# A decode step on one core: TensorE's program made shorter with register-addressed loops, q and h computed with the weights as stationary operand, one V buffer

## The chip, the cores and the metric

The kernel runs on one core of a Trainium2 chip. The metric is the device time of one execution in microseconds (us), lower is better. The kernel before takes 112.35 us (median of three runs, 112.1 to 112.72). In the later sections it was run again beside every experiment on the same chip, and its medians there are 111.36 to 112.28. Because of this spread, I give for every experiment its excess: its median less the median of the kernel before in the same call.

TensorE is the matrix engine. The profile shows its work as loads of a stationary operand ("load") and matmuls that stream a moving operand through it ("matmul"), 558 of each in the kernel before; one load and one matmul are called a pair here, and one run through a loop's body a pass. The granted clock is the share of TensorE's full clock that the profile shows it to have had. VectorE does the elementwise work, the transposes and the copies out of the accumulators in these kernels. A transfer queue (SP in the profile) issues the loads from memory.

## The reference, cut to what matters

```python
def reference(A_x, A_k_cache, A_v_cache, A_wq, A_wo, B_x, B_w1, B_w2):
    # B=2, Sq=1, D=448, 16 query heads, 8 K/V heads, Dh=256; the last W=2048 keys of 8192
    xn = _layernorm(A_x)
    q = (xn @ wq)                       # 448 x 4096
    scores = einsum(q, k[-2048:]) / 16
    o = softmax(scores) @ v[-2048:]
    s = o.reshape(B, 1, 4096) @ wo      # 4096 x 448
    g = silu(relu(xn @ w1) @ w2)        # the FFN: 448 x 1792, 1792 x 448
    return A_x + s * g
```

Nearly all of the work is reading 44 MB: 16.8 MB of K, 16.8 MB of V, and 10.6 MB of wq, w1, w2 and wo.

## The kernel before

The keys and values are treated in four units u = 0 to 3 of 4.2 MB of K and 4.2 MB of V each (one batch element, four K/V heads). For each unit VectorE transposes K (T), TensorE makes the scores (S), softmax follows, TensorE spreads P over the partitions (the P products), and P times V (PV) is summed. TensorE's part of a unit is one body of a loop over "turns", in which PV lags by one turn and the small products after PV (turn, spread) by two. A token is a semaphore that is counted down when it is taken, so that the same wait can stand in every turn.

The products of q, of h (x times w1) and of F (h times w2) have x or h as the small stationary operand and the weights as the moving one, 448 or 512 columns at a time:

```python
        def load_v(u, cuts=(0, NT)):          # units 0 to 2 in vbuf[0], unit 3 in vbuf[1], where wq was
            deps = [None if u == 0 else st["q_mm"] if u == NU - 1 else st["PV", u - 1]]
            ...
        d_wq = [pr.dma(SP, wq_sb[:, 0:FIRST * HC], wq_src[:, 0:FIRST * HC])]       # 2/7 of wq
        load_k(0)
        d_wq.append(pr.dma(SP, wq_sb[:, FIRST * HC:SLOTS * HC], wq_src[:, FIRST * HC:SLOTS * HC]))
        load_k(1)
        load_v(0)
        st["w1"] = pr.dma(...)                # right behind V0
        st["w2"] = pr.dma(...)
        ...
            for x in range(4):                # softmax(u): the P products, 16 pairs, written out
                for g in range(4):
                    lo = 128 * (4 * x + g)
                    o = pr.op(PE, mm(view(pbk, 2 * x, [[8, 16], [1, 2]]), spread[:, lo:lo + 128], ...
        ...
        def do_q():                           # 28 pairs, written out
            for s in range(SLOTS):
                for i in range(4):
                    lo = s * HC + i * 512
                    o = pr.op(PE, mm(obk[32 * i:32 * i + 4, :], xr[:, 4 * s:4 * s + 4], wq_sb[:, lo:lo + 512], ...
        ...
            if u == 1:                        # the FFN stands at the end of turn 1
                pr.group = "ffn"
                do_H()                        # 28 pairs
                do_F()                        # 14 pairs
        ...
        turn(3)
        v_f = pr.op(DVE, ...)
        idle_loop(5, 2)                       # ten matmuls whose result nobody reads
        do_PV(3, (0, 1))
        attend_turn(2)
        do_PV(3, (2,))
        attend_spread(2)
        do_PV(3, (3,))
        ...
        idle_work(1)
        ...
        idle_work(3)
```

Of the kernel before, what the change touches and what calls it, by code (L numbers as in the profile page):

```python
# [14 lines left out]
class _Op:  # L15
    __slots__ = ("eng", "fn", "deps", "dma", "needed", "value", "sem", "turn", "group", "token", "gives")

    def __init__(self, eng, fn, deps, dma):
        self.eng, self.fn, self.deps, self.dma = eng, fn, deps, dma
        self.needed, self.value, self.sem = dma, 0, None  # L20
        self.turn, self.group, self.token, self.gives = None, None, None, False


class _Prog:
# [4 lines left out]
    def __init__(self, nc, es):  # L29
        self.nc, self.es = nc, es  # L30
        self.lists = {PE: [], DVE: [], ACTE: [], SP: [], POOL: []}
        self.turn, self.group, self.runs = None, None, {}

    def op(self, eng, fn, deps=(), token=None):
        o = _Op(eng, fn, [d for d in deps if d is not None], False)
        if eng == PE:
            o.turn, o.group, o.token = self.turn, self.group, token
        self.lists[eng].append(o)
        return o
# [6 lines left out]
    def run(self, turns):  # L46
# [6 lines left out]
        taken = {DVE: [], SP: []}  # L53
        for o in pe:
            if o.token is not None:
                assert not o.token.gives
                o.token.gives = True
                taken[o.token.eng].append(o.token)
        for e in taken:
            assert taken[e] == [o for o in self.lists[e] if o.gives]  # L60
# [16 lines left out]
        for e, ops in self.lists.items():  # L77
            sem, count = self.es.enter_context(nc.semaphore(f"s_{e}")), 0
            for o in ops:
                if o.gives:  # L80
                    assert o.dma or not o.needed
                    o.sem = give[e]
                elif o.dma:
                    n += 1
                    o.sem, o.value = self.es.enter_context(nc.semaphore(f"d_{n}")), 16
                elif o.needed:
                    count += 1
                    o.sem, o.value = sem, count
# [22 lines left out]
        for eng, name in ((nc.vector, "dve"), (nc.tensor, "pe")):  # L111
            again[name] = eng.alloc_register(f"{name}_again")
            nc.br("dve_all" if name == "dve" else "pe_visit", engines=[eng.engine])
# [15 lines left out]
        body = [o for o in loop if o.turn == turns - 1]  # L129
        body += [o for o in loop if o.group == "ffn"]  # L130
        with nc.body("pe_all", parent=main, valid_engines=[t.engine]):
            top = nc.cur_bb
# [3 lines left out]
            with t.Fori(0, turns) as i:  # L136
                k = 0
                while k < len(body):
                    g = body[k].group
                    end = next((m for m in range(k, len(body)) if body[m].group != g), len(body))  # L140
                    part, runs = body[k:end], self.runs[g]
                    k = end
                    if runs == list(range(turns)):
                        emit(t, part, seen)
                    elif len(runs) == 1:
                        with t.If(i == runs[0]):
                            emit(t, part, seen)
                    else:
                        assert runs == list(range(runs[0], turns))
                        with t.If(i > runs[0] - 1):  # L150
                            emit(t, part, seen)
            nc.br("pe_past", engines=[t.engine])
            nc.switch_bb("pe_visit", parent=main)
            t.nop()
            nc.br("pe_all", engines=[t.engine])
            nc.switch_bb("pe_past", parent=top)
# [5 lines left out]
def bass_recurrent_scan__sliding_block_cached__dense_activation_relu__decode_kernel(  # L162
# [29 lines left out]
    TILED = 9  # L192
    NWO = 16
    FIRST = 2
# [4 lines left out]
    with es:  # L199
# [21 lines left out]
        qrep = named("qrep", [128, 128], BF)  # L221
# [9 lines left out]
        q_n = named("q_n", [128, 512], BF)  # L231
        qz = named("qz", [128, 4 * 64], BF)
        h_n = named("h_n", [128, FC // 4], BF)
        h_t = named("h_t", [128, FC // 4], BF)
# [13 lines left out]
        q_t = named("q_t", [128, 512], F32)  # L248
# [16 lines left out]
        obk_last = psum("obk_last", [128, 512], F32)  # L265
# [28 lines left out]
        def load_v(u, cuts=(0, NT)):  # L294
            deps = [None if u == 0 else st["q_mm"] if u == NU - 1 else st["PV", u - 1]]
            d_v[u] = []
            for lo, hi in zip(cuts, cuts[1:]):
                d_v[u].append((hi, pr.dma(SP, vbuf[u // (NU - 1)][:, lo * DH:hi * DH],
                                          kv_src(u, A_v_cache)[:, :, lo * DH:hi * DH], deps)))

        d_wq = [pr.dma(SP, wq_sb[:, 0:FIRST * HC], wq_src[:, 0:FIRST * HC])]
        load_k(0)
        d_wq.append(pr.dma(SP, wq_sb[:, FIRST * HC:SLOTS * HC], wq_src[:, FIRST * HC:SLOTS * HC]))
        load_k(1)
        load_v(0)
        st["w1"] = pr.dma(SP, w1_sb[:, 0:W2_AT], w1_src)
        st["w2"] = pr.dma(SP, w2_sb[:, W2_AT:W2_AT + 14 * D].rearrange("p (hf f) -> p hf f", hf=2), w2_src)
# [5 lines left out]
        p_z = [pr.op(POOL, lambda e, t=t: e.memset(t[:, :], 0.0)) for t in (qrep, spread, sel, h_z, at_z)][-1]  # L313

        a_z = [pr.op(ACTE, lambda e, t=t: e.memzero(t[:, :])) for t in (obk, sbk, hbk, fbk, obk_last)][-1]
# [48 lines left out]
        for s in range(SLOTS):  # L364
            m_xr = pr.op(PE, mm(mbk_ap(2 * s, 2), xg[0:B, 128 * s + 128:128 * s + 256], ident[0:B, 0:B], s == 0),
                         [v_xn, p_id])
# [4 lines left out]
        v_qr = pr.op(DVE, lambda e: e.tensor_copy(  # L371
            view(qrep, 0, [[32, 4], [4, 4], [1, 4]]), view(ident, 0, [[0, 4], [32, 4], [1, 4]])), [p_z])
# [20 lines left out]
        def turn_q(u):  # L393
            b, v = divmod(u, 2)
            for r in range(2):
                st["q"] = pr.op(DVE, lambda e, r=r: e.tensor_tensor(  # L396
                    out=view(qz, r, [[64, 4], [8, 8], [2, 4]]), in0=view(q_t, 256 * r + 2 * v + b, [[4, 4], [32, 8], [0, 4]]),
                    in1=view(gmask, 0, [[0, 4], [0, 8], [1, 4]]), op=ALU.mult), [st["q_t"], v_gm, st.get(("S", u - 1, NBLK - 1))])

        def softmax(u):  # L400
# [9 lines left out]
            for x in range(4):  # L410
                for g in range(4):
                    lo = 128 * (4 * x + g)
                    o = pr.op(PE, mm(view(pbk, 2 * x, [[8, 16], [1, 2]]), spread[:, lo:lo + 128],
                                     view(et, 512 + 2 * g, [[32, 16], [1, 2]]), g == 0, g == 3), token=token)
                    token = None
# [7 lines left out]
        def out_bank(u):  # L423
            return obk if u < NU - 1 else obk_last

        def do_PV(u, gs=range(4)):
            bank, src = out_bank(u), vbuf[u // (NU - 1)]
            for g in gs:
                deps, token = [], None
                if u == NU - 1:  # L430
                    deps = [next(d for hi, d in d_v[u] if hi >= 16 * g + 16), st["pt", u]]
                elif g == 0:
                    token = d_v[u][0][1]
                for a in range(2):
                    for i in range(4):
                        t = 16 * g + 4 * i + 2 * a
                        o = pr.op(PE, mm(bank[32 * i:32 * i + 16, :],
                                         pt[:, 8 * t:8 * t + 16], src[:, t * DH:(t + 2) * DH],
                                         g == 0 and a == 0, g == 3 and a == 1, tile_position=(0, 32 * i)), deps, token=token)
                        deps, token = [], None  # L440
            st["PV", u] = o

        def attend_scale(u):
            st["osb", u] = pr.op(DVE, lambda e: e.tensor_scalar(  # L444
                out=o_sb[:, :], in0=view(out_bank(u), 0, [[1, 512]]), scalar1=rs[:, u:u + 1], scalar2=None, op0=ALU.mult),
                [st["PV", u], st["rs", u], st.get(("oT", u - 1))])

        def attend_turn(u):
            deps = [st["osb", u]] if u > 1 else []
            for dhi in range(2):  # L450
                for tp in range(2):
                    o = pr.op(PE, mm(mbk_ap(136 + 8 * dhi, 8), o_sb[:, 256 * tp + 128 * dhi:256 * tp + 128 * dhi + 128],
                                     fold[:, 8 * tp:8 * tp + 8], tp == 0, tp == 1), deps)
                    deps = []
# [6 lines left out]
        def attend_spread(u):  # L461
# [3 lines left out]
                                      [at] if u > 1 else [], token=None if u > 1 else at)  # L465
# [3 lines left out]
        def do_q():  # L469
            deps = d_wq + [v_xr, a_z]  # L470
            for s in range(SLOTS):
                for i in range(4):
                    lo = s * HC + i * 512
                    o = pr.op(PE, mm(obk[32 * i:32 * i + 4, :], xr[:, 4 * s:4 * s + 4], wq_sb[:, lo:lo + 512],
                                     s == 0, s == SLOTS - 1, tile_position=(0, 32 * i)), deps)
                    deps = []
            st["q_mm"] = o
            v = pr.op(DVE, lambda e: e.tensor_scalar(
                out=q_n[:, :], in0=obk[:, :], scalar1=SCALE, scalar2=None, op0=ALU.mult), [o])
            m = pr.op(PE, mm(pbk[:, :], qrep[:, :], q_n[:, :], True, True), [v, v_qr])  # L480
            st["q_t"] = pr.op(DVE, lambda e: e.transpose(view(q_t, 0, [[1, 512]]), view(pbk, 0, [[64, 8], [1, 2], [2, 32]])), [m])

        def do_H():
            deps = [st["w1"]]
            for s in range(SLOTS):
                for i in range(4):
                    lo = s * FC + i * (FC // 4)
                    o = pr.op(PE, mm(hbk[32 * i:32 * i + 4, 0:FC // 4], xr[:, 4 * s:4 * s + 4], w1_sb[:, lo:lo + FC // 4],
                                     s == 0, s == SLOTS - 1, tile_position=(0, 32 * i)), deps)
                    deps = []  # L490
            v = pr.op(DVE, lambda e: e.tensor_scalar(
                out=h_n[:, :], in0=hbk[:, 0:FC // 4], scalar1=0.0, scalar2=None, op0=ALU.max), [o])
# [153 lines left out]
```

## Time and profile before

| | kernel before |
|---|---|
| median time | 112.35 us |
| profiled span, granted TensorE clock | 109.8 us, 0.891 |
| bytes moved by the load queue | 44.11 MB, busy 95% of the span |
| TensorE busy / VectorE busy | 55% / 57% |
| instructions executed | 1368 |
| K2, V1 and K3 issued at | 36.7, 54.3 and 54.9 us |

The page's head and the waits are read in the prediction below. Some more lines are from the timeline of TensorE; the columns are start, duration, engine, line, operation, output<-inputs, shapes and count, and in brackets the idle time before it with what ended it.

```profile
22.78 3.16 PE L361 MATMUL obk<-vbuf,xr 128*4 128x512 bf16 x28 [13.91 <-DMA vbuf<-in_A_wq_dram]
...
56.43 0.84 PE L361 MATMUL hbk<-wf,xr 128*4 128x224 bf16 x28
59.00 1.66 PE L361 MATMUL fbk<-wf,h_z 128*2 128x448 bf16 x14 [1.73 <-DVE h_z L494]
...
94.52 2.32 PE L361 MATMUL wbk<-q_n,ident 128*128 128x512 bf16 x10
...
103.20 4.79 PE L361 MATMUL hbk<-kbuf,at_z 128*8 128x112 bf16 x92
```

The first line is q (28 pairs in 3.16 us), the second h, the third F. The whole FFN takes 4.2 us (56.43 to 60.66) including VectorE's steps between them. It costs nothing there: the transposes of K2, next in VectorE's order, begin at 59.51, as soon as K2 has landed. The fourth line is the ten idle matmuls, the last the products with wo that end the kernel, 52 ns each.

### The profile page before, as it was taken

What the parts mean: (1) busy time and instruction counts of PE and PEld (TensorE: products, weight loads), DVE (VectorE), ACT (ScalarE), POOL (GpSimd) and SP (SyncE); (2) the same over time, 40 slices, a digit from 0 to 9 for tenths busy, and PEclk for the clock granted to TensorE, in tenths of its full rate; (3) what the DMA queues carried; (4) which work ended last, traced back from release to release, by engine and by line L of the source; (5) the groups of instructions that cost most, each with busy time, mean ns of one, the idle gap of its engine ahead of it and who ended that gap; (6) DMA issues with size and microseconds to landing.
All of it is one profiled execution on the core that took longest, in us unless ns stands there. A gap on an engine that the chain in (4) does not pass through costs nothing. (4 is left out here: it accounts for less than half of the span.)

```text
span 109.8 us, 1368 instructions
## 1 busy us (share of the span) xinstructions
PE 60.4 (55%) x558; PEld 19.5 (18%) x558; DVE 63.0 (57%) x96; ACT 10.2 (9%) x19; POOL 3.1 (3%) x11
## 2 busy tenths in 40 slices
PE   0001000076599330899755597853039785898993
PEld 0000000020111020000241010112001011534792
DVE  0249109995400459993468999266299926624601
ACT  4990000000000110000200000020000002000000
POOL 7400000000000000000000000000000000000000
PEclk9999999999999995579996569997555899999999
DMA  3998989998899889998899999999999999899950
GB/s 60 502 388 382 549 371 395 439 537 382 382 453 501 382 367 416 411 548 382 382 501 394 406 406 465 441 406 406 465 441 406 444 430 430 361 419 410 402 207 7
DMA packets 3046, 44.15 MB, mean 402 GB/s; under 512 B 354, under 2 KB 612, under 8 KB 1508
## 3 DMA queue, kind: packets, MB, share of 16 engines
q1 hardware_dynamic: 3008, 44.11, 95.0%
q8 instruction: 2, 0.03, 0.1%
q10 hardware_dynamic: 36, 0.01, 0.1%
HBM read 44.11 MB, written 0.00 MB: 402 GB/s over the span
## 5 line engine op out<-in xcount | busy, mean ns | idle before, releaser
L379 DVE STREAM_TRANSPOSE kt<-kbuf 128x2048 f32<-128x2048 f32 x16 | 35.9, 2286 | 7.8 <-DMA kbuf<-in_A_k_cache_dram 7.8
L361 PE MATMUL sbk<-kt,qz 128*8 128x512 bf16 x128 | 31.1, 1073 | 13.6 <-PEq L102 13.5
L401 DVE TENSOR_REDUCE rm<-sbk 128x1 f32<-128x512 f32 x4 | 2.8, 692 | 14.6 <-PE sbk L361 14.6
L361 PE MATMUL obk<-vbuf,xr 128*4 128x512 bf16 x28 | 3.2, 626 | 13.9 <-DMA vbuf<-in_A_wq_dram 13.9
L407 ACT ACTIVATE et<-sbk,bias 128x512 bf16<-128x512 f32 x4 | 2.7, 687 | 81.1 <-DVE bias L405 81.1
L361 PEld LDWEIGHTS sbk<-kt,qz 128*8 128x8 bf16 x128 | 2.6, 87 | 28.9 <-issue 28.7
L361 PE MATMUL pbk<-et,spread 128*128 128x32 bf16 x64 | 2.6, 193 | 7.2 <-PEq L102 7.2
L361 PE MATMUL obk<-vbuf,pt 128*16 128x512 bf16 x96 | 5.8, 381 | 0.0
L361 PE MATMUL mbk<-ident,xg 2*128 2x2 bf16 x7 | 0.3, 163 | 8.5 <-DVE xg L325 8.5
L361 PE MATMUL wbk<-q_n,ident 128*128 128x512 bf16 x15 | 4.1, 395 | 1.4 <-DVE qz L396 1.4
L361 PE MATMUL hbk<-kbuf,at_z 128*8 128x112 bf16 x92 | 4.8, 213 | 0.0
L409 DVE STREAM_TRANSPOSE et<-et 128x512 bf16<-128x512 bf16 x4 | 2.8, 712 | 3.4 <-ACT et L407 3.4
L417 DVE TENSOR_TENSOR pt<-pbk,hmask 128x512 bf16<-128x512 f32 x4 | 2.8, 692 | 3.3 <-PE pbk L361 3.3
L361 PEld LDWEIGHTS hbk<-kbuf,at_z 128*8 128x8 bf16 x92 | 4.6, 87 | 0.1
L361 PEld LDWEIGHTS pbk<-et,spread 128*128 128x128 bf16 x64 | 2.2, 99 | 10.5 <-issue 10.5
L361 PEld LDWEIGHTS obk<-vbuf,pt 128*16 128x16 bf16 x96 | 2.5, 94 | 6.8 <-issue 4.7
L361 PEld LDWEIGHTS obk<-vbuf,xr 128*4 128x4 bf16 x28 | 0.8, 114 | 15.4 <-issue 15.4
L611 DVE TENSOR_TENSOR tmp<-hbk,g_sb 8x112 f32<-8x112 f32 x1 | 0.3, 262 | 4.4 <-PE hbk L361 4.4
L361 PE MATMUL fbk<-wf,h_z 128*2 128x448 bf16 x14 | 1.7, 567 | 1.7 <-DVE h_z L494 1.7
L456 DVE TENSOR_TENSOR at_exp<-mbk,qmask 128x128 bf16<-128x128 f32 x4 | 1.2, 292 | 2.5 <-PE mbk L361 2.5
L361 PE MATMUL obk_last<-vbuf,pt 128*16 128x512 bf16 x32 | 2.3, 380 | 0.0
L444 DVE TENSOR_SCALAR o_sb<-obk,rs 128x512 bf16<-128x512 f32 x3 | 2.2, 731 | 0.0
(80 smaller groups left out, 43.9 us busy)
## 6 DMA issues: line engine op xcount, KB each, us to landing
kbuf<-in_A_k_cache_dram SPq DMA_DIRECT2D x4, 4096.0 KB, 23.4
vbuf<-in_A_v_cache_dram SPq DMA_DIRECT2D x3, 4096.0 KB, 15.8
wf<-in_B_w_dram SPq DMA_DIRECT2D x2, 1568.0 KB, 42.4
vbuf<-in_A_v_cache_dram SPq DMA_DIRECT2D x1, 3072.0 KB, 22.5
vbuf<-in_A_wq_dram SPq DMA_DIRECT2D x1, 2560.0 KB, 20.9
vbuf<-in_A_wq_dram SPq DMA_DIRECT2D x1, 1024.0 KB, 6.1
vbuf<-in_A_v_cache_dram SPq DMA_DIRECT2D x1, 1024.0 KB, 24.4
kbuf<-in_A_wo_dram SPq DMA_DIRECT2D x1, 1008.0 KB, 26.2
```

Source lines behind the costliest of these rows:

```text
L361: return lambda e: e.matmul(out_ap, lhsT=lhsT, rhs=rhs, start=start, stop=stop, skip_group_check=True, **kw)
L379: st["kt", u, blk] = pr.op(DVE, lambda e: e.transpose(view(dst, 0, [[1, 32 * NT]]), view(src, 32 * blk, [[DH // 2, NT], [1, 32]])), [d_k[u ...
L401: v = pr.op(DVE, lambda e: e.tensor_reduce(out=rm[:, :], in_=sbk[:, :], axis=AX.X, op=ALU.max), [st["S", u, NBLK - 1]])
L407: a = st["exp", u] = pr.op(ACTE, lambda e: e.activation(e_sb, sbk[:, :], ACT.Exp, bias=bias[:, 0:1], accum_out=ssum[:, 0:1]), [v, st.get(( ...
L409: token = pr.op(DVE, lambda e: e.transpose(e_t, e_sb), [a, st.get(("Pt", u - 1))])
L417: st["pt", u] = pr.op(DVE, lambda e: e.tensor_tensor(out=view(pt, 0, [[8, NT], [2, 4], [1, 2]]), in0=view(pbk, 0, [[2, NT], [0, 4], [1, 2] ...
L444: st["osb", u] = pr.op(DVE, lambda e: e.tensor_scalar(out=o_sb[:, :], in0=view(out_bank(u), 0, [[1, 512]]), scalar1=rs[:, u:u + 1], scalar ...
L456: st["at", u] = pr.op(DVE, lambda e: e.tensor_tensor(out=view(at_exp, 0, [[16, 8], [8, 2], [1, 8]]), in0=view(mbk, 136, [[1, 8], [8, 2], [ ...
L611: v_t = pr.op(DVE, lambda e: e.tensor_tensor(out=tmp[:, :], in0=hbk[0:NROW, 0:NCOL], in1=g_sb[:, :], op=ALU.mult), [m_o, v_g])
```

## The change

Its intent is a shorter program of TensorE (178 matmuls as built, for 322) and so fewer instruction fetches. Five things follow from it:

1. The P products, q, h and F become loops whose operands are addressed through registers.
2. q and h are computed with the weights as stationary operand (128 columns with a stride of 2 or 7 elements) and x as the moving one, four columns wide. q so needs 112 pairs instead of 28, h 49 instead of 28, F 56 direct pairs instead of 14 tiled ones. (Tiled products write to four groups of partitions side by side, and a later "fold" sums the four; direct ones all add to one result.) The small loop that turns x, seven pairs, becomes one of these too.
3. There is one V buffer, so V3 too waits for PV of the unit before. wq is loaded whole ahead of K0. w1 and w2 are loaded behind V2.
4. The FFN moves to turn 4, ahead of PV of unit 3. The small products become two more turns of the loop.
5. The idle matmuls go. 16 of wo's products are tiled instead of 9, and 64 direct ones remain instead of 92.

```diff
+        def looped(n, body, deps=(), token=None):
+            def fn(e):
+                with e.Fori(0, n) as i:
+                    o = body(e, i)
+                return o
+            return pr.op(PE, fn, deps, token, times=n)
...
-        def load_v(u, cuts=(0, NT)):
-            deps = [None if u == 0 else st["q_mm"] if u == NU - 1 else st["PV", u - 1]]
+        def load_v(u):
+            deps = [st["PV", u - 1] if u else None]
...
-        d_wq = [pr.dma(SP, wq_sb[:, 0:FIRST * HC], wq_src[:, 0:FIRST * HC])]
+        d_wq = pr.dma(SP, wq_sb[:, 0:SLOTS * HC], wq_src)
         load_k(0)
-        d_wq.append(pr.dma(SP, wq_sb[:, FIRST * HC:SLOTS * HC], wq_src[:, FIRST * HC:SLOTS * HC]))
         load_k(1)
         load_v(0)
...
-            for x in range(4):
+            def body(e, x):
                 for g in range(4):
-                    lo = 128 * (4 * x + g)
-                    o = pr.op(PE, mm(..., spread[:, lo:lo + 128], ...
+                    m = mm(view(pbk, 2 * x, [[8, 16], [1, 2]]), view(spread, 512 * x + 128 * g, [[1, 128]]), ...)(e)
+                return m
+            o = looped(4, body, token=token)
...
         def do_q():
+            def body(e, s):
+                with e.Fori(0, 4) as h:
+                    for g in range(2):
+                        for par in range(2):
+                            o = mm(view(hbk, 16 * h + 4 * (2 * g + par), [[1, 4]]),
+                                   view(wq_sb, HC * s + 512 * h + 256 * g + par, [[2, 128]]), view(xr, 4 * s, [[1, 4]]), False)(e)
+                return o
+            o = looped(SLOTS, body, [d_wq, v_xr, a_z])
...
         def do_H():
+            def body(e, s):
+                for j in range(7):
+                    o = mm(view(hbk, 64 + 4 * j, [[1, 4]]), view(w1_sb, FC * s + j, [[7, 128]]), view(xr, 4 * s, [[1, 4]]), False)(e)
+                return o
+            o = looped(SLOTS, body, [st["w1"]])
...
         def do_F():
+            st["F"] = looped(14, lambda e, f: direct(e, fbk, h_z, w2_sb, f * GAP, f * D + W2_AT), [st["w2"], st["h"]])
...
+            if u == NU:
+                pr.group = "ffn"
+                do_H()
+                do_F()
...
         load_v(2)
+        load_ffn()
...
-        idle_loop(5, 2)
-        do_PV(3, (0, 1))
...
+        turn(NU)
+        turn(NU + 1)
```

## The prediction

> **What bounds the kernel now.** I read the page's head first: which resource is full.
>
> ```profile
> span 109.8 us, 1368 instructions
> ...
> DMA  3998989998899889998899999999999999899950
> ...
> q1 hardware_dynamic: 3008, 44.11, 95.0%
> ```
>
> The transfers are busy from the second slice to the last but two; TensorE has 55% and VectorE 57%. So the stream of 44.11 MB decides, if it has no holes. To test that I laid the landings (the issue time in the timeline plus "us to landing" of the table of DMA issues) against the bytes queued up to each. K0 (the first K load; 5.24 MB with what is ahead of it) landed at 1.17 + 15.4 = 16.6 us, the rest of wq (7.86 MB) at 1.83 + 20.9 = 22.7, V0 (16.25 MB) at 4.43 + 37.7 = 42.1, K3 (32.05 MB) at 78.95, where VectorE's wait for it ends. All lie within 0.3 us of 4.4 + MB/0.430. The full 44.11 MB then give 107.0 us, and the half-microsecond windows show the last traffic in 106.5 to 107.0. So there is no hole, and 107 us is a floor [...]; behind it come only 2.8 us.
>
> Next, the transfer queue's own instructions and waits, because what is issued late makes a hole:
>
> ```profile
> 36.73 0.55 SPq L42 DMA_DIRECT2D kbuf<-in_A_k_cache_dram  x1
> 54.34 0.54 SPq L42 DMA_DIRECT2D vbuf<-in_A_v_cache_dram  x1
> 54.92 0.60 SPq L42 DMA_DIRECT2D kbuf<-in_A_k_cache_dram  x1
> ```
> ```profile
> SPq L42 <- PE obk L361: 34.4, 2, 17.3
> SPq L42 <- PE sbk L361: 30.5, 1, 30.5
> ```
>
> K2 waits 30.5 us for the scores of unit 0 (kbuf is reused), V1 waits 17.3 us for PV of unit 0 (vbuf is reused). Neither costs anything now: when K2 is issued at 36.7, V0, w1 and w2 are still to come (w2 lands at about 49.7), and when V1 is issued at 54.3, K2 lands only at 59.5. But the margin at V1 is just 5.2 us, and the 3.2 MB of w1 and w2, 7.5 us of traffic, are what makes it.
>
> Then the timeline of the start, for the chain that issues these two:
>
> ```profile
> 16.61 8.89 DVE L379 STREAM_TRANSPOSE kt<-kbuf 128x2048 f32<-128x2048 f32 x4 [5.30 <-DMA kbuf<-in_A_k_cache_dram]
> ...
> 25.99 0.69 DVE L478 TENSOR_SCALAR q_n<-obk 128x512 bf16<-128x512 f32 x1 [0.49 <-PE obk L361]
> ...
> 29.24 7.45 PE L361 MATMUL sbk<-kt,qz 128*8 128x512 bf16 x32
> ...
> 36.73 0.55 SPq L42 DMA_DIRECT2D kbuf<-in_A_k_cache_dram  x1
> ...
> 39.78 0.65 PE L361 MATMUL pbk<-et,spread 128*128 128x32 bf16 x16 [3.09 <-PEq L102]
> ...
> 41.54 8.88 DVE L379 STREAM_TRANSPOSE kt<-kbuf 128x2048 f32<-128x2048 f32 x4
> ```
>
> K0 transposed (8.9 us), q made, scores (7.45 us), softmax with the spreading of P (0.65 us on TensorE), K1 transposed (8.9 us), scores and PV. From K2's issue to V1's issue this takes 54.34 - 36.73 = 17.6 us.
>
> [...] the instruction queue moved two packets, and the stream that sets the end has no hole that a stall of TensorE could have made. [...]
>
> **The change part by part.**
>
> Instruction fetch: the build has 322 matmuls in TensorE's program before and 178 after. Worth 0 on this path.
>
> The start. wq now comes whole ahead of K0, so K0 has 7.86 MB up to its end and lands at 22.7 us instead of 16.6. Its transposes end at 22.7 + 8.9 = 31.6. In VectorE's order they stand ahead of the scaling of q, so however early q's products are ready, q follows at 31.6. The tiles are smaller (64 columns for 512) and the idle matmul is gone, so I allow 1.9 us instead of the 3.25 from 25.99 to 29.24. Scores run from 33.5 to 33.5 + 7.45 = 40.9, and K2 is issued at 41.0 instead of 36.7.
>
> The q loop: 28 inner passes of four matmuls; in the built program each matmul has an instruction that works out addresses in registers, and each pass has an add and a branch. Twenty-eight pairs of load and matmul of the FFN took 0.84 us before, 0.03 us each. For an addressed pair I estimate 0.10 us and for a pass 0.15 [...]. 28 x 0.55 + 7 x 0.2 = 16.8 us from wq's landing at 12.9: it ends at 29.7, hidden behind the transposes. At 0.15 per pair it would end near 36 and cost 4.
>
> Hole one: V0 has 16.25 MB up to its end and lands at 42.2. A transfer issued at t into an empty queue lands about 2.8 us + bytes/0.430 later (an estimate between 3.66, the 4.4 less the first issue at 0.74, and 2.2 if only the late engines count). K2: 41.0 + 2.8 - 42.2 = 1.6 us hole; it lands at 53.6.
>
> Hole two: V1 is issued 17.6 us after K2, plus the longer P loop: 4 x (4 x 0.10 + 0.15) = 2.2 us for 0.65, so 1.5 more, plus some 0.5 for the token waits: 60.6. 60.6 + 2.8 - 53.6 = 9.8 us hole. This is the largest certain loss: w1 and w2 have left, and everything is 4.3 us later.
>
> Later units: V2 would be issued near 80.7, K3 lands at 83.0: just no hole. V3 needs PV of unit 2, near 100.7, against w2's landing at 100.7: a hole of up to 2.8. The stream ends at 107.0 + 1.6 + 9.8 + 2.8 = 121.2, about 121 to 122.
>
> The FFN now stands ahead of the last PV in TensorE's order. It starts after softmax of unit 3 and its turn, near 107, and takes 7 x (7 x 0.10 + 0.15) = 6.0 for h and 14 x (4 x 0.10 + 0.15) = 7.7 for w2, so it ends near 121.4 with its VectorE step. V3 lands at 113.3, so the FFN, not V3, releases PV(3): 123.6. From there to the end the kernel before took 109.8 - 99.2 = 10.6 us; now there are fewer direct products (64 for 92) but seven more tiled ones: 9.9. Span 133.5, and with the 2.55 by which the median time exceeded the span (112.35 - 109.8): about 136. I take 135.
>
> **The rivals.** (a) Cheap addresses, 0.05 us per pair: P costs 0.8 more, the FFN ends near 112, and the stream bounds the end: about 122 to 125 of span, 125 to 127 measured. For it: loads and matmuls were issued at 0.03 us a pair. (b) Dear addresses, 0.2 us and more per pair: q ends at 44, delaying scores by 11 us; each P loop costs 4, and the FFN takes 26: 160 and up. For it: each address instruction carries three to seven additions or shifts. (c) The transfers stay fed: if the 1.6 and 9.8 us holes closed, the end would be 107 + 2.8 and nothing would change, about 112. Against it: the 17.6 us chain is measured and w1 and w2 are plainly gone from that place. (d) A gain through fewer fetches: at most what follows the last landing, 2.8 us, could shrink; I see 1 us at best.
>
> **Range and chances.** The holes alone add some 10 to 14 us; the cost per addressed pair, which no row of the profile before gives, spreads the rest from 125 to over 160. I take 119 to 160. Faster by over 2% would need a time under 110.1, below the floor plus its tail: 1%. Within 2% needs both holes closed and the FFN hidden: 4%. Slower: 95%.
>
> **What will show it.** K2 issued near 41 and V1 near 60 with a drop of the DMA line between some 51 and 62 shows the holes; V1 issued before 50 refutes me. The mean spacing of q's 112 small matmuls gives the cost per pair: 0.15 us with all overhead would be my middle, over 0.25 is rival (b). TensorE busy with w1 and w2 after V3 has landed shows the FFN step. If the DMA line is full up to the end and the last landing still comes at 107, the argument of the two holes was wrong.

## The result, and the profile after

The changed kernel takes 175.53 us (median of four runs, 175.14 to 176.49) against 112.22 us for the kernel before in the same call. The ratio is 1.568, with a 95% interval of 1.554 to 1.581. A ratio is computed here as the mean time of one kernel's fast runs over that of the other's fast runs in the same rounds, so it is not quite the ratio of the medians. The excess is 63.3 us.

The page of the changed kernel, head and groups (for a group: line, engine, operation, operands, count, then busy us and mean ns, then the idle time before it and what ended most of it):

```profile
span 174.2 us, 2136 instructions
...
PEclk9999999999999995599755696579955555555559
DMA  6999899990000079500998979899399991000000
...
q1 hardware_dynamic: 2960, 44.11, 60.5%
...
L360 PE MATMUL hbk<-xr,vbuf 128*128 x112 | 18.2, 184 | 19.5 <-issue 18.4
...
L360 PE MATMUL pbk<-et,spread 128*128 128x32 bf16 x64 | 9.6, 198 | 13.9 <-PEq L105 8.6
```

The same 44.11 MB now fill 60% of the span, and the DMA line has three stretches of zeros: five slices of 4.36 us from about 39 to 61 us, two before 83 us, and everything from about 145 us to the end. The stream does not set the end any more. The fifth line names the first cause: 112 matmuls of q were busy for 18.2 us, and ahead of them TensorE stood idle for 19.5 us, of which 18.4 are put down to "issue", that is, to nothing that the profile shows it waiting for.

The transfer queue's waits (us in total, times, longest) and its timeline answer to those of the prediction:

```profile
SPq L45 <- PE obk L360: 58.1, 3, 20.5
SPq L45 <- PE sbk L360: 57.0, 1, 57.0
```
```profile
60.94 0.53 SPq L45 DMA_DIRECT2D kbuf<-in_A_k_cache_dram  x1
81.98 0.54 SPq L45 DMA_DIRECT2D vbuf<-in_A_v_cache_dram  x1
...
102.79 0.54 SPq L45 DMA_DIRECT2D vbuf<-in_A_v_cache_dram  x1
...
123.61 1.20 SPq L45 DMA_DIRECT2D vbuf<-in_A_v_cache_dram  x2
```

K2 is issued at 60.9 us (36.7 before), after a wait of 57.0 us for the scores of unit 0. V1, V2 and V3 follow at intervals of about 20.8 us.

The start, from the timeline:

```profile
16.40 0.67 PE L360 MATMUL hbk<-xr,vbuf 128*128 x4 [0.57 <-issue]
...
21.79 8.89 DVE L385 STREAM_TRANSPOSE kt<-kbuf 128x2048 f32<-128x2048 f32 x4 [7.97 <-DMA kbuf<-in_A_k_cache_dram]
...
49.97 0.64 PE L360 MATMUL hbk<-xr,vbuf 128*128 x4 [0.61 <-issue]
50.65 0.23 DVE L478 TENSOR_SCALAR q_n<-hbk 128x64 bf16<-128x64 f32 x1 [19.96 <-PE hbk L360]
...
53.52 7.37 PE L360 MATMUL sbk<-kt,qz 128*8 128x512 bf16 x32 [2.20 <-PEq L105]
...
65.42 0.58 PE L360 MATMUL pbk<-et,spread 128*128 128x32 bf16 x4 [0.42 <-issue]
```

The first and third lines are two of q's 28 passes, each four matmuls: 0.67 us of work after a gap of 0.57. A pass begins every 1.25 us (16.40 less the start of the one before, 15.19, is 1.21; others are 1.23 and 1.26), and every fourth one 1.68 us after the last, where the outer loop turns. The loop ran from 13.9 to 50.6 us, 36.7 us. K0's transposes were done at 30.7, and the scaling of q waited another 19.96 us for the products. The last line is one of the four passes of a P loop.

And the end:

```profile
140.46 0.96 PE L360 MATMUL hbk<-xr,wf 128*128 x7 [0.44 <-issue]
...
156.72 0.70 PE L360 MATMUL fbk<-wf,h_z 128*8 x4 [0.44 <-issue]
...
157.94 3.59 PE L360 MATMUL obk<-vbuf,pt 128*16 128x512 bf16 x32 [0.52 <-PEq L105]
...
167.77 4.53 PE L360 MATMUL hbk<-kbuf,at_z 128*8 128x112 bf16 x64
```

The first two are the last pass of h (seven pairs every 1.40 us) and of F (four pairs every 1.12 us). The FFN ran from 132.0 to 157.4 us with no other engine's work beside it, and from about 145 us on without transfers either: everything had landed. Then PV of unit 3 took 3.59 us, where PV of unit 2 had taken 1.92: the granted clock was 0.50 (157.9 to 161.6 us) for 1.00 (100.8 to 102.7). Two windows of TensorE show the clock, third from the end of the line:

```profile
13.00:51.00 38.00, 18.30 (x114) 11.73 (x115) 9.94 (x8) 0.00 (x0) 0.00 (x0) 1.00 0.71 304
...
132.00:157.50 25.50, 16.67 (x105) 10.81 (x105) 0.25 (x1) 0.04 (x1) 0.00 (x0) 0.50 0.47 195
```

It was 1.00 through all of q's loop and 0.50 through the FFN. In windows of half a microsecond it fell at 126 us, in the P loop of unit 3 and so ahead of the FFN, and rose again only at 170.

### The profile page after: what moved, and what is told of

Same layout as the page of the kernel before. It is cut to its first block, busy times and chain, and to the rows that moved or that the text cites. A ratio compares the mean times of both kernels' runs of the same rounds, so it can differ in the third digit from the quotient of the medians.

```text
span 174.2 us, 2136 instructions
## 1 busy us (share of the span) xinstructions
PE 97.5 (56%) x664; PEld 45.0 (26%) x664; DVE 61.3 (35%) x93; ACT 10.6 (6%) x20; POOL 3.0 (2%) x10
## 3 DMA queue, kind: packets, MB, share of 16 engines
q1 hardware_dynamic: 2960, 44.11, 60.5%
HBM read 44.11 MB, written 0.00 MB: 253 GB/s over the span
## 5 line engine op out<-in xcount | busy, mean ns | idle before, releaser
L360 PE MATMUL sbk<-kt,qz 128*8 128x512 bf16 x128 | 31.0, 1070 | 12.3 <-PEq L105 12.3
L360 PE MATMUL hbk<-xr,vbuf 128*128 x112 | 18.2, 184 | 19.5 <-issue 18.4
L360 PEld LDWEIGHTS hbk<-xr,vbuf 128*128 x112 | 11.7, 104 | 26.1 <-issue 21.6
L360 PE MATMUL pbk<-et,spread 128*128 128x32 bf16 x64 | 9.6, 198 | 13.9 <-PEq L105 8.6
L360 PE MATMUL fbk<-wf,h_z 128*8 x56 | 10.0, 251 | 6.0 <-issue 5.3
L360 PEld LDWEIGHTS pbk<-et,spread 128*128 x64 | 6.5, 102 | 19.9 <-issue 18.1
L360 PE MATMUL obk<-vbuf,pt 128*16 128x512 bf16 x128 | 9.3, 443 | 0.5 <-PEq L105 0.5
L360 PE MATMUL hbk<-xr,wf 128*128 x49 | 6.7, 208 | 3.2 <-issue 3.2
L360 PEld LDWEIGHTS fbk<-wf,h_z 128*8 x56 | 4.6, 83 | 11.3 <-issue 8.3
L360 PEld LDWEIGHTS hbk<-xr,wf 128*128 x49 | 6.2, 131 | 3.7 <-issue 3.6
L360 PEld LDWEIGHTS obk<-vbuf,pt 128*16 128x16 bf16 x128 | 3.6, 102 | 9.1 <-issue 7.0
(70 smaller groups left out, 44.3 us busy)
## 6 DMA issues: line engine op xcount, KB each, us to landing
vbuf<-in_A_v_cache_dram SPq DMA_DIRECT2D x3, 4096.0 KB, 12.4
wf<-in_B_w_dram SPq DMA_DIRECT2D x2, 1568.0 KB, 16.5
```

What stands on the lines that cost most here:

```text
L360: return lambda e: e.matmul(out_ap, lhsT=lhsT, rhs=rhs, start=start, stop=stop, skip_group_check=True, **kw)
```

## The experiments

Eighteen kernels ran, all free of what a check for races can find; an earlier build of one, e11, was refused for a race on a token that two transfers shared, and was mended before it ran (of that build nothing is kept). Each is an edit of the changed kernel unless its text says otherwise. "Unrolled" always means:

```diff
-            o = looped(n, body, ...)
+            o = unrolled(n, body, ...)     # for i in range(n): body(e, i); all addresses are constants
```

Medians are over the fast runs. e8, e12 and e13 had one slow run each and e17 two, of 4, 6, 4 and 6; all others had none.

| run | what it is | median us | excess us | ratio |
|---|---|---|---|---|
| after | the changed kernel | 175.53 | 63.3 | 1.568 |
| e1 | q unrolled | 157.26 | 45.2 | 1.406 |
| e2 | h and F unrolled | 154.39 | 42.3 | 1.377 |
| e3 | P unrolled | 161.47 | 49.4 | 1.441 |
| e4 | all register-addressed loops unrolled | 124.23 | 12.2 | 1.108 |
| e5 | only w1 and w2 loaded early | 174.84 | 63.5 | 1.567 |
| e6 | q: 7 passes of 16 pairs | 155.42 | 44.1 | 1.389 |
| e7 | q: loops kept, fixed addresses | 155.63 | 44.3 | 1.391 |
| e8 | e4 with w1 and w2 early | 120.74 | 9.4 | 1.086 |
| e16 | e4 with wq in two parts | 119.54 | 8.0 | 1.067 |
| e9 | e4 with both, the load order of before | 118.30 | 6.7 | 1.059 |
| e10 | e9 with the FFN in turn 2 | 127.06 | 15.2 | 1.137 |
| e13 | e8 with the FFN in turn 2 | 131.72 | 19.9 | 1.178 |
| e11 | e10 with V3 in its own buffer | 121.78 | 10.0 | 1.091 |
| e14 | e9 with V3 in its own buffer | 118.52 | 7.0 | 1.061 |
| e15 | e14 with the FFN after turn 1 | 117.74 | 6.2 | 1.053 |
| e17 | e15 with the idle matmuls | 115.72 | 3.4 | 1.029 |
| e12 | the kernel before, 16 tiled products | 111.58 | -0.2 | 1.001 |
| e18 | the kernel before, no idle matmuls | 111.98 | -0.3 | 0.998 |

### One loop at a time: e1, e2, e3, and all: e4

> Only the q loop of the changed kernel is written out (112 matmuls with fixed addresses, the same weights as stationary). Theory 1 (the cost is the addressed loop: 0.13 to 0.16 us per pair of weight load and matmul and 0.5 to 0.65 us per pass): q takes 7 to 12 us instead of 36.7, ends before K0's transposes do (near 31), and the time falls by 20 us, to 154 to 157. Theory 2 (the order of the transfers and the one V buffer are the cause): less than 5 us saved. Theory 3 (weights as stationary with strided columns are dear in themselves): q still takes over 25 us and less than 10 us is saved.

```diff
-                with e.Fori(0, 4) as h:
+                for h in range(4):
...
-            o = looped(SLOTS, body, [d_wq, v_xr, a_z])
+            o = unrolled(SLOTS, body, [d_wq, v_xr, a_z])
```

The timeline of e1 has q in one line:

```profile
13.34 3.13 PE L360 MATMUL hbk<-xr,vbuf 128*128 128x4 bf16 x112 [0.37 <-DVE xr L380]
```

The same 112 pairs with the same strided weights as stationary operand take 3.13 us, 0.028 us each, and so as long in all as the 28 wide ones of before (3.16 us). The weights as stationary operand cost nothing here; the loop costs 36.7 - 3.1 = 33.6 us. K0's transposes then hide q fully, q is scaled at 31.6 instead of 50.65 us, and the time falls by 63.3 - 45.2 = 18.1 us. (In this build most passes of the P loop took 1.10 to 1.15 us instead of 1.00 to 1.08, though nothing in them had changed. I cannot explain that.)

> Only the two FFN loops are written out (49 and 56 matmuls). Theory 1: the FFN takes 6 to 8 us instead of 25.4; V3 lands near 136, so PV of unit 3 starts some 19 us earlier and the time falls to 155 to 158. Theory 2: under 5 us saved. Theory 3: the 49 loads of h alone still take 10 us, 7 to 10 us saved in all.

```profile
132.28 2.77 PE L360 MATMUL hbk<-xr,wf 128*128 128x4 bf16 x49
...
135.47 4.59 PE L360 MATMUL fbk<-wf,h_z 128*8 128x112 bf16 x54 [0.43 <-DVE h_z L500]
```

h took 2.77 us and F about 4.6, the FFN with VectorE's step from 132.3 to 140.0 us instead of 132.0 to 157.9. PV of unit 3 took 1.89 us instead of 3.59. In all 21.0 us: 18.2 are the FFN's, and 1.7 of the rest are PV of unit 3, which ran at a higher clock. The granted clock had fallen here too, at about 129 us, but at about 139 us, some 3.5 us into F's unbroken products, it rose again, in time for PV. (The page's clock line reads 8, 5, 5, 8 and 9 tenths in its slices of 3.84 us from 126.6 us on; the two times are estimates from these.) So h's pairs took 0.057 us each at a granted clock of 0.50, where q's in e1, of the same shape, took 0.028 at 0.9 or more (clock line of e1's page).

> Only the P loop is written out. It takes 4.1 us four times now and 0.65 before; it lies in the chain from one unit's scores to the next unit's transposes. Theory 1: four times 3.4 saved, 13 us, time 161 to 164. Theory 2: units wait for transfers, 0 to 4 us saved.

The P products took 0.65 us again, as before the change, for 4.1 in the loop (3.7 for its four passes, and they begin 0.37 us later after the scores). Four units by 3.45 us are 13.8; measured 13.9. All four lie on the chain, since the transfers no longer cover it.

> All register loops written out, with the changed order of transfers, one V buffer and weights as stationary kept: what is left of the change without its loops. Theory 1: 20 + 19 + 13 us fall away, then the two holes of the transfers that I predicted (1.6 and 9.8 us) set the end: 121 to 126 us, K2 issued near 40, V1 near 58 with the DMA line empty behind it. Theory 2: about 160 and over. Theory 3: 140 to 150.

51.1 of the 63.3 us go. (The small loop that turns x is written out here too.) The three alone sum to 18.1 + 21.0 + 13.9 = 53.0, so they hardly overlap: they stand one after the other on one chain. The bytes, the load order and the single V buffer are those of the changed kernel, and the DMA line is filled almost throughout again:

```profile
DMA  6999999999898098930398989798989999899910
```

The low slices at about 40 to 43 and 55 to 64 us (slices of 3.07 us) are the two holes that the prediction saw; the runs with other load orders below close them. The chain that ended last in e4 waits for wo's landing again ("96.55 16.60 DMA" of wo, then 6 us of products), as in the kernel before.

### What in a loop is dear: e6, e7

> q in 7 passes of 16 addressed matmuls instead of 28 passes of 4 in two nested loops. If a pass costs 0.65 us and a pair 0.155: 7 x (16 x 0.155 + 0.65) = 22 us, q ends near 36, 14 us saved, 160 to 163. If the cost were all per pass: 9 us, hidden, 20 saved (155). If it were all per addressed pair: no change (175).

```diff
-                with e.Fori(0, 4) as h:
+                for h in range(4):
...
-            o.times = 4 * SLOTS
```

```profile
18.79 2.13 PE L360 MATMUL hbk<-xr,vbuf 128*128 x16 [0.44 <-issue]
```

With 16 pairs in a pass, a pass takes 2.57 us: 2.13 us for 16 pairs, 0.133 us each, and a gap of 0.44. So there are two costs, one for each pair and one for each pass. With passes of 4, the gap is 0.57 and four pairs take 0.67. (The edit also takes one of the two loop variables out of the addresses; what that alone gave was not parted from the longer pass.) q now ended at 31.2 us, sooner than I had expected, just when K0's transposes do, and the time fell by 19.2 us, as with full unrolling.

> The q loop with its 28 passes of 4 matmuls kept, but all of them at fixed addresses (the same weights again and again: wrong on purpose, since q is not q). If working out and using register addresses is the cost: a pass falls from 1.25 to 0.4 to 0.6 us, q takes 11 to 17 us, hidden behind the transposes, and the time is that of the written-out q, 154 to 157. If the branch of the loop is the cost: a pass stays above 1 us, time near 170 to 175.

```diff
-    o = mm(view(hbk, 16 * h + 4 * (2 * g + par), ...), view(wq_sb, HC * s + 512 * h + 256 * g + par, ...), view(xr, 4 * s, ...), ...)
+    o = mm(view(hbk, 4 * (2 * g + par), ...), view(wq_sb, 256 * g + par, ...), view(xr, 0, ...), ...)
```

This kernel computes a wrong q: it has the two nested loops with the same 28 passes, but constant addresses. The comparison with the reference passed all the same, so it says little about q. Its timeline:

```profile
15.38 1.44 PE L360 MATMUL hbk<-xr,vbuf 128*128 128x4 bf16 x16 [0.49 <-issue]
...
21.11 0.25 PE L360 MATMUL hbk<-xr,vbuf 128*128 128x4 bf16 x4 [0.44 <-issue]
...
21.55 1.05 PE L360 MATMUL hbk<-xr,vbuf 128*128 128x4 bf16 x12 [0.20 <-issue]
```

In the second and third line one pass stands by itself, and the next begins 0.44 us later, after a gap of 0.20; other neighbours are 0.41 and 0.42 us apart. An inner pass so falls from 1.25 us to about 0.42, and all 28 take 13.0 us. They still have their counting and their branches. So these are the smaller part: of the 33.6 us that q's loop costs, 13.0 - 3.1 = 9.9 stay, and 36.7 - 13.0 = 23.7 came with the addresses in registers. This run does not part the arithmetic on the registers from the reading of operand addresses out of them, and it was made for q alone; that P, h and F divide in the same way is not shown.

### The order of the loads: e5, e8, e16, e9

> The changed kernel with w1 and w2 loaded again right behind V0, loops kept. Theory 1: the transfers wait for the compute chain and not the reverse, so nothing moves: 174 to 177. Theory 2 (the hole that w1 and w2 left): 10 us saved, about 165.

```diff
-        load_ffn()                      # behind V2
+        st["w1"] = pr.dma(...)          # right behind V0, as in the kernel before
+        st["w2"] = pr.dma(...)
```

No change: 63.5 us of excess for 63.3. While the loops rule, the chain does not wait for the transfers of K2 and K3, and 7.5 us of bytes more or less ahead of them are nothing.

> All loops written out and w1, w2 behind V0 again; one V buffer kept. Closes the hole at V1 (w2 lands near 50, K2 near 59.5, V1 issued near 58.5: at most 2 us) but opens one at V3, which must wait for PV of unit 2 after V2's landing near 91 with nothing queued in between: about 5 us. Span 115 to 118, time 116 to 120, against 121 to 126 of the version with w1, w2 behind V2. If the holes were no cause, no difference between the two.

The same edit on e4 is worth 12.2 - 9.4 = 2.8 us. Once the loops are gone the order counts.

> All loops written out and wq cut in two around K0 as before; w1, w2 behind V2 and one V buffer kept. K0 lands near 16, the scores of unit 0 end near 37 instead of 42, V1 is issued near 54.5 instead of 59.7; K2 lands near 52, so a hole of some 5 us stays at V1 where there were 11 in all. Span 116 to 119 (122.8 with wq whole). If the late K0 costs nothing: 122 to 123.

```diff
-        d_wq = pr.dma(SP, wq_sb[:, 0:SLOTS * HC], wq_src)
+        d_wq = [pr.dma(SP, wq_sb[:, 0:2 * HC], wq_src[:, 0:2 * HC])]
         load_k(0)
+        d_wq.append(pr.dma(SP, wq_sb[:, 2 * HC:SLOTS * HC], wq_src[:, 2 * HC:SLOTS * HC]))
```

wq in two parts around K0, on e4: K2 is issued at 36.9 instead of 42.2 us, V1 at 54.5 instead of 59.7, and 4.2 us are gained. A hole at 50.5 to 55.5 us remained, as w1 and w2 still came late.

> All loops written out, wq cut in two and w1, w2 behind V0, so the order of the transfers of the kernel before, with one V buffer and the FFN in turn 4. No hole at V1; V3 waits for PV of unit 2 (V2 lands near 89): V3 issued near 92.5, 5 to 6 us empty, last landing near 113. Span 115 to 118. If the order of the transfers were all: 110 to 112.

Both together: V1 is issued at 54.3 us, to the tenth as in the kernel before, and there is no hole before it. Another 1.2 us. V3 waits for PV of unit 2 and is issued only at 91.2; the queue is empty for some four us before that.

### The FFN in another turn, V3 in its own buffer: e10, e13, e11, e14, e15

> All loops written out; wq cut in two as before, w1 and w2 behind V0, the FFN in turn 2; of the change only the one V buffer and the weights as stationary are left. If the late start of the scores and the missing 3.2 MB make the hole at V1, it is gone: V1 issued near 54, K2 landing near 59.5. The hole at V3 stays, since V3 waits for PV of unit 2, which waits for V2's landing near 89: V3 issued near 92, 4 to 6 us empty. Span 113 to 116, time 115 to 118. If one V buffer costs nothing: 112.

```diff
-            if u == NU:
+            if u == 2:
                 pr.group = "ffn"
...
-        pr.runs = {... "ffn": [4], ...}
+        pr.runs = {... "ffn": [2], ...}
```

> All loops written out, w1 and w2 behind V0, wq still whole ahead of K0, and the FFN moved from in front of the last PV to turn 2. In the version with the FFN in turn 4 (121.3) TensorE's 8 us of FFN stood between softmax and PV of unit 3 and the chain that ended last was TensorE's. Now the transfers with their two holes (2 us at V1, 5 to 6 at V3) set the end: span 116 to 118, time 117 to 120. If the place of the FFN costs nothing: 121.

Both missed: 8.5 us slower than e9 and 10.5 slower than e8. VectorE's timeline in e10 says why:

```profile
68.58 0.26 DVE L528 TENSOR_TENSOR g_sb<-fbk,tmp 8x112 f32<-8x112 f32 x1
68.77 8.87 DVE L392 STREAM_TRANSPOSE kt<-kbuf 128x2048 f32<-128x2048 f32 x4
```

The moved FFN brought its VectorE steps along, and they stand in VectorE's order ahead of the transposes of K2. Those now begin at 68.77 us; in e9 they begin at 59.08. VectorE waited for TensorE's FFN and TensorE then for VectorE. That was a fault of my edit, and it says nothing of the change.

> The one before, with V3 in the second buffer again, so that it is queued early. If the hole at V3 was all that was left, the stream has no hole, the last landing is at 107 and the time is that of the kernel before, 111 to 113; the smaller work behind the last landing could give up to 0.5 us. If weights as stationary cost something in themselves, it stays above 114.

```diff
+            buf = vbuf[u // (NU - 1)]                     # unit 3 where wq was
-            deps = [st["PV", u - 1] if u else None]
+            deps = [st["q_mm"] if u == NU - 1 else st["PV", u - 1] if u else None]
```

On e10 this gained 5.3 us, but with the same fault in it (transposes at 69.04), so it fell short of what I had expected too.

> The one before with V3 in the second buffer and so queued early: no hole, last landing at 107. What is left is the FFN in turn 4 on TensorE, 8 us between the softmax of unit 3 (near 95) and PV of unit 3, which ends near 106 instead of 99; from there 10 us: span 114 to 118, the chain that ended last TensorE's. If the place of the FFN costs nothing: 110.

The same edit on e9, with the FFN back in turn 4. The DMA lines of e9 and of e14:

```profile
DMA  4999899998999999989989999899970389899960
```
```profile
DMA  3999899989989799998998989999899999980000
```

The hole before V3 is gone, and the stream ends some 6 us sooner. The time is the same (7.0 us of excess for 6.7): in turn 4 the FFN keeps TensorE from 95.9 to 103.7 us, PV of unit 3 comes after it, and the products with wo after that. The buffer had no cost of its own left behind this.

> The one before with the FFN right behind unit 1's softmax and the turn and spread steps between the score blocks, as the kernel before has them. Only q and h by weights as stationary, F by direct products and the shorter end are left of the change. Theory: nothing of the 12 us remains, last landing at 107, span 110 to 112, time 111 to 114 (the end may run at the lower clock, since the idle matmuls are gone). If weights as stationary cost something: over 115.

```diff
-            if u == NU:
+            if u == 1:
+                attend_scale(0)
                 pr.group = "ffn"
                 do_H()
                 do_F()
...
+                    if u > 1 and blk == 1:  # turn and spread between the score blocks, as before
```

(The loop of turns was rewritten for this: every part of a turn now stands in two conditions of its own, and the small products of units 0 and 1 stand among the scores.) Here VectorE's last FFN steps stand after the turns, and the FFN, at 53.9 to 62 us, costs nothing: VectorE waits 2.08 us for K2's landing and begins its transposes at 59.32, in the kernel before at 59.51. The stream ends at about 105 us, without a hole (from 105 to 110 us 0.1 MB moved), so the prediction's 107.0 us was no floor. Still it is only 0.8 us faster than e14, and I had expected 111 to 114 us. The end ran at a low clock:

```profile
98.04 3.59 PE L349 MATMUL obk<-vbuf,pt 128*16 128x512 bf16 x32 [0.81 <-issue]
...
109.28 4.99 PE L349 MATMUL hbk<-kbuf,at_z 128*8 128x112 bf16 x64
```

The granted clock from 100 to 110 us was 0.50 (0.77 from 110 to 116), and the last products took 78 ns each, where the kernel before needs 52 (4.79 us for 92).

### The idle matmuls: e17 and e18

> e15_ffn_after_turn_1 with the 14 idle matmuls of the kernel before put back (ten ahead of PV of unit 3, one before the products with wo, three before the fold). e15 was 117.7 us, and its last 15 us ran at the granted clock 0.5: PV of unit 3 3.59 us, tiled products 1.66, fold 1.66, direct products 78 ns each. If the missing idle matmuls are what let the clock fall, these become about 1.9 to 2.3, 0.9, 0.9 and 52 ns, and the time falls by 3 to 5 us to 112 to 115, near the kernel before (about 111.9). If the clock falls for another reason (a rest of the chain, or the transposes before it), the groups stay at their long times and the time stays at 117 to 119.

```diff
+            if u == NU:
+                pr.group = "idle"
+                idle_loop(5, 2)
...
+        idle_work(1)                    # ahead of the products with wo
...
+                idle_work(3)            # ahead of the fold
```

```profile
98.69 1.90 PE L349 MATMUL obk<-vbuf,pt 128*16 128x512 bf16 x32 [0.81 <-issue]
...
104.83 1.66 PE L349 MATMUL tbk<-kbuf,at_z 128*2 128x448 bf16 x16
...
109.27 3.91 PE L349 MATMUL hbk<-kbuf,at_z 128*8 128x112 bf16 x64
```

With the ten idle matmuls ahead of it PV of unit 3 took 1.90 us for 3.59 (granted clock from 95 to 100 us 1.00, in e15 0.58). But from 102.4 to 104.3 us TensorE had nothing to do, the clock fell to 0.50 from 105 to 110, and the tiled products and the fold still took 1.66 us each. It gains 2.7 us by the excess and is 2.9% slower than the kernel before.

> The same question from the other side: the kernel before without its idle matmuls (the loop of ten, the one and the three), nothing else. If they hold the clock up at the end, the last products (92 in 4.79 us at 52 ns) slow to about 78 ns each, the fold and PV of unit 3 double, and the time rises by 2 to 5 us to 114 to 117. If the clock does not depend on them, it stays within 0.5 us of the kernel before.

```diff
-        idle_loop(5, 2)
-        idle_work(1)
-        idle_work(3)
```

The kernel before does without them: ratio 0.998 (0.994 to 1.003). The clock did fall from 95 to 100 us, to 0.66 on average (1.00 in the kernel before), and the matmuls of PV of unit 3 took 3.41 us for 2.26. But there the products with wo wait for wo's landing at about 101 us anyway, and from 100 us on the clock was up again (1.00): the last 92 products took 4.69 us. So in these two kernels the idle matmuls are worth something only where TensorE itself sets the end (2.7 us in e17; nothing that the interval would show in e18).

### e12

> The kernel before with 16 instead of 9 of the 32 wo rows as tiled products, the part of the change that shortens the end: 64 direct products instead of 92. The last landing stays at 107; at best 0.5 us saved (111.6), at worst the sums come later and nothing is saved. A version that beats both kernels clearly is not expected, because the stream ends at 107.

```diff
-    TILED = 9
+    TILED = 16
```

The kernel before with the changed kernel's number of tiled products is the same (ratio 1.001, 0.994 to 1.007). In the kernel before, this part of the change costs nothing and gains nothing that the interval of 0.7% would show.

No experiment beats the kernel before; e12 and e18 equal it.

## Why the prediction was right or wrong

The direction was right, and the size was not: 135 us with a range of 119 to 160 stood against 175.5. The steps of the prediction, as its text has them, against the trace (spans; the 40.7 us at the end are the whole error):

| step | predicted | measured | error so far | added by this step |
|---|---|---|---|---|
| K2 issued | 41.0 | 60.9 | 19.9 | 19.9 |
| V1 issued | 60.6 | 82.0 | 21.4 | 1.5 |
| V3 issued | 100.7 | 123.6 | 22.9 | 1.5 |
| FFN begins | 107 | 132.0 | 25.0 | 2.1 |
| FFN ends, PV of unit 3 begins | 121.4 | 157.9 | 36.5 | 11.5 |
| end of the span | 133.5 | 174.2 | 40.7 | 4.2 |

**The step that failed is "For an addressed pair I estimate 0.10 us and for a pass 0.15".** Both figures were estimates of mine that no row of the profile before backed. From them came "28 x 0.55 + 7 x 0.2 = 16.8 us", hidden behind the transposes. The loop took 36.7, and the scaling of q waited 19.96 us for it. The runs show in its place about 0.13 us for an addressed pair (e6) against 0.028 for one with constant addresses (e1), and 0.42 to 0.57 us for a pass against the 0.15 assumed (e6, and the lines of q, h, F and P in the profile after). The form of the sum holds only roughly with these figures: 7 pairs by 0.13 and a gap of 0.44 to 0.5 are 1.35 to 1.41, and h's passes took 1.40; but 4 pairs by 0.13 and a gap of 0.57 are 1.09, and q's passes took 1.25. The pair was only 30% off; the pass was off by a factor of three to four, and more than half of a pass of four pairs is not its pairs: of q's 1.25 us they are 0.53. My 0.15 for a pass was meant for its branch alone. e7 shows that this was half right: with constant addresses the pass has its branch, and its gap is 0.15 to 0.20 us. The rest comes with register addresses, for which I had no row.

The same two figures carry the other terms: "2.2 us" for a P loop was 4.1, and "7 x (7 x 0.10 + 0.15) = 6.0 for h and 14 x (4 x 0.10 + 0.15) = 7.7 for w2" was 25.4 in all. By experiment the loops of q, P and the FFN cost 18.1, 13.9 and 21.0 us.

**Rival (b) had the path and nearly the size.** By the prediction's own sign, a mean spacing of q's matmuls over 0.25 us, it was the case: 36.7 us for 112 are 0.33. It put each P loop at 4 us and the FFN at 26, both right, and q's end at 44, still 6.6 us too early. But it laid the cost on the pair (0.2 us and more), where most of it was the pass, so that its right figures are partly luck. I gave it too little room in the range, though the text said that no row of the profile before gave the cost. That was the point to widen the upper end.

**The two holes were there, but not as causes.** "1.6 us" at K2 was about 22 (no traffic from 40 to 62 us), and "9.8" at V1 was about 11 (72 to 83 us). Holes that wide are here the mark of a chain that no longer depends on the transfers: after q it ran from one unit to the next in 20.8 us, more than the 19.5 us (8.39 MB at 430 GB/s) that the bytes of a unit need. e5 shows it: w1 and w2, loaded early, went into the first hole, the second stayed 11 us wide, and the time did not change. The estimate for a transfer into an empty queue, 2.8 us + bytes/0.430, was good: it gives 12.6 us for 4.19 MB, and from issue to landing K2 took 12.4 and V1 12.3 in the profile after. The argument of the holes was made for a kernel bound by the stream, and in that kernel, e4, it was good: K2 issued at 42.2 (predicted 41.0), V1 at 59.7 (60.6, of which 1.5 are for the longer P loop, which e4 no longer has, and 0.5 for the token waits, an estimate of mine that no row backed), holes of 2 and 7.5 us, the last traffic at 117.0 us instead of 106.5, excess 12.2 us, where the prediction gave "some 10 to 14 us" to the holes alone.

**The tail was longer than "9.9" after PV of unit 3.** From the start of PV(3) to the end were 2.2 + 9.9 = 12.1 us predicted and 16.3 measured. After the looped FFN the granted clock was 0.50: PV of unit 3 took 3.59 us, PV of unit 2 1.92 at 1.00, and the tiled products took 1.67 us, in e14 0.93 at 1.00. In e2 the clock had fallen ahead of the FFN too, and it rose some 3.5 us into F's unbroken products, while in the loops, with a gap in every pass (matmuls busy 16.7 of 25.5 us), it stayed at 0.50. I had not put this into the sum. What made it fall is open: q's loop, with matmuls busy half the time (18.3 of 38.0 us), ran at 1.00 throughout, and in e1 TensorE stood idle from 16.5 to 31.9 us at a recorded clock of 0.9 or more.

**"Instruction fetch: worth 0"** is not contradicted. All of e4's register-addressed loops are unrolled, its instruction queue moved two packets where the changed kernel moved one, and it is 51 us faster. What fewer fetches gain by themselves was not isolated.

**What the other 12 us of e4 are.** Late K0 behind the whole of wq: 4.2 (e4 to e16). w1 and w2 behind V2: 1.2 (e16 to e9) or 2.8 (e4 to e8). The remaining 6.7 of e9 have no one owner. Taking away V3's wait alone gave nothing (e14), because the FFN's place in turn 4 bound the end; moving the FFN too gave 0.8 (e15), because the end ran at half clock; the idle matmuls gave 2.7 more (e17). Each removal uncovered the next. The last 3.4 us of e17 I only read from its trace: PV of unit 3 begins at 98.7 us instead of 96.8, since the small products of unit 2 now stand ahead of it and not among it, and 1.86 us lie between the last small product and the next matmul, where TensorE leaves the loop of turns. I take most of that gap for a cost of my own edit with its many conditions, since in the changed kernel the gap at this place is 0.55 us. This was not tested.

## What to carry to other kernels

Before writing a TensorE loop whose operands are addressed through registers, measure one pass: here a pair with constant addresses took 0.028 us, an addressed one 0.13 (e1 and e6, both at a granted clock of 0.9 or more), and each pass another 0.42 us and more, so q's loop ran twelve times slower than the same pairs written out (36.7 us for 3.1), and F's over three times (15.2 us for 4.6). Putting more pairs into a pass (e6) took off 19.2 us, as much as writing the loop out (e1, 18.1), where the loop had other work to hide behind, so look first at what it can hide behind. And when several costs stand in series with something that hides them, removing them one at a time shows little: e14 gained nothing and e15 0.8 us, because the next one was right behind.
